# Sixteen weight loads moved from SyncE's DMA queue to GpSimd's, in a kernel that runs a delta-rule attention and an MLP

## The chip, the cores and the metric

The kernel runs on one core of a Trainium2 chip. The metric is the device time of one execution in microseconds (us). A core has five engines with an instruction queue each: TensorE (PE in the profile; its weight loads are PEld), VectorE (DVE), ScalarE (ACT), GpSimd (POOL) and SyncE (SP). Each takes its instructions strictly in order and waits at an instruction until the semaphores that it names have been raised. Transfers between DRAM and the on-chip memory are started by an instruction on SP's, ACT's or POOL's queue and then run by themselves.

## The reference

All inputs are float32 but for the two weight matrices: the set-up scales them by a float64 number, which makes them float64 arrays.

```python
# q, k, v: (4, 8, 768, 48); beta: (4, 8, 768)
k_n = k / (np.linalg.norm(k, axis=-1, keepdims=True) + 1e-06)
state = np.zeros((B, H, D, D))
for t in range(S):
    kt, vt, bt = (k_n[:, :, t], v[:, :, t], beta[:, :, t, None])
    y[:, :, t] = np.einsum('bhd,bhde->bhe', q[:, :, t], state)
    v_old = np.einsum('bhde,bhd->bhe', state, kt)
    state = state + bt[:, :, :, None] * np.einsum('bhd,bhe->bhde', kt, vt - v_old)
x = y.transpose(0, 2, 1, 3).reshape(3072, 384)
h = x @ w_in                                  # w_in: (384, 2048)
g = h * np.clip(h + 3.0, 0.0, 6.0) / 6.0
out = (g @ w_out).astype(np.float32)          # w_out: (2048, 384)
```

## The kernel before

**Tiling.** The 768 tokens are cut into 24 chunks of 32. A chunk of all 4 batches fills 128 partitions (4 x 32). For a chunk the kernel normalizes k (`norms`, then the product `kb` in `prep`, line 496, on POOL), transposes k and q on PE (line 510, tile pt), copies them to the tile KQ on ACT (line 518), forms scores (line 533, tile sc), inverts a small triangular matrix per head, and runs the chain over the state (`chain`: matmul pz at line 813, its copy R on ACT at line 913, the state update su at line 924). Each two chunks make one block of 256 rows for the MLP: `up` (line 980, tile ph) multiplies by w_in, `down` (line 1140, tile po) and for later blocks `down_by_seven` (line 1204) by w_out.

**Weights.** They come as float64 and there is no float64 arithmetic, so they are loaded as pairs of 32-bit words and converted on the chip. The two matrices are cut into 16 pieces: 8 of w_in (384 rows x 256 columns) and 8 of w_out (256 rows x 384 columns), each 768 KB in DRAM. `load_w(i)` (line 312) starts the transfer of piece i into a raw buffer; there are six such buffers, in the tile `spare` and in parts of the tile `w_out` that are not yet in use, and the table `frees` says which earlier piece must have been converted before a buffer is used again. The conversion of a piece is

- three ACT instructions (`scales`, line 337): line 348 scales the high word in its place, line 351 makes a half-precision value of it, line 353 scales the low word; the last two write a carry into `spare`;
- one VectorE shift (`convert`, line 368), from the high word to the final place;
- one GpSimd addition (line 375), which adds the carry there.

**Order.** All of it is recorded under a manual schedule. The string `ORDER` (lines 23 to 41) gives the opening word by word, where `w` stands for the start of one weight piece, `a` for one ACT instruction of `scales`, `c` for one step of `convert`, `k`, `q` and `v` for one load of 48 KB each, and so on; after it a loop over chunks with a table of steps goes on. An engine executes its instructions in the order in which they were recorded. Where a DMA is recorded on a queue, it therefore stands among the other instructions of that engine: on SP among the loads of k, q and v and the stores of the output, on POOL among the masks (line 472), the products (lines 484 and 496), the memsets (lines 277, 285 and 677) and the additions (line 375). In the recorded order the 16 starts stand early: the first before kb's first product, the last after the masks that POOL makes about 112 us into the run before.

DMAs of one queue also share eight semaphores in turn, so the ninth waits until the first has landed; SP's and ACT's DMAs take theirs from one set of eight, GpSimd's would take them from a set of its own.

The lines around the change, without the branch for float32 weights:

```python
raws = []
for i, n in enumerate((0, 1, 2, 3, 4, 5, 0, 1, 3, 4, 5, 0, 1, 5, 0, 1)):
    s, f = weights[i][0].shape[1:]
    raws.append(homes[n].bitcast(U32).rearrange("p (s f z) -> p s f z", s=s, z=2))
frees = {6: 0, 7: 1, 8: 3, 9: 4, 10: 5, 11: 6, 12: 7, 13: 10, 14: 11, 15: 12}
```

Of the kernel before, what the change touches and what calls it, by code (L numbers as in the profile page):

```python
# [44 lines left out]
def kernel(  # L45
# [21 lines left out]
    nc = tc.nc  # L67
# [69 lines left out]
    def needs(*what):  # L137
        assert past.issuperset(what), (what, set(what) - past)
# [173 lines left out]
    def load_w(i):  # L312
        dst, src = weights[i]
        if src.dtype == FP32:
            if i >= NWI:
                needs(("w", NWI - 1))
            nc.sync.dma_start(out=dst, in_=src)
            past.add(("raw", i))
            return
        if i in frees:  # L320
            needs(("seen", frees[i], 0), ("seen", frees[i], 1))
        past.add(("raw", i))
        nc.sync.dma_start(
            out=raws[i].rearrange("p s f z -> p s (f z)"), in_=src.bitcast(U32)
        )

# [1025 lines left out]
    def pieces():  # L1352
        for i in range(NW):
            load_w(i)
            yield
# [166 lines left out]
```

## Time and profile before

| what | value |
|---|---|
| median of 3 runs | 669.1 us (668.65 to 669.87) |
| the profiled execution | 669.61 us, its span 667.8 us |
| PE busy | 635.8 us (95%) |
| VectorE (DVE) busy | 462.8 us (69%) |
| ScalarE (ACT) busy | 260.5 us (39%) |
| GpSimd (POOL) busy | 227.5 us (34%), 336 instructions |
| DMA queue of SP | 31.29 MB in 88,128 packets |
| DMA queue of ACT | 0.30 MB |

The span is what lies between the first and the last instruction of the profiled execution; 1.8 us of its time lie around it. A row of the timeline reads: start in us, duration in us, engine, line of the kernel, operation, output<-input with their shapes, how many merged instructions; in brackets, how long the engine stood idle just before it and what ended that. A `q` behind an engine's name is its instruction queue: the row "SPq L323" is SP starting the DMA of line 323, which takes part of a microsecond; the data land later. The page lists the time from that start to the landing for each kind of DMA:

```profile
spare<-in_moe_w_in_dram SPq DMA_DIRECT2D x4, 768.0 KB, 6.1
w_out<-in_moe_w_in_dram SPq DMA_DIRECT2D x4, 768.0 KB, 6.4
w_out<-in_moe_w_out_dram SPq DMA_DIRECT2D x4, 768.0 KB, 6.9
spare<-in_moe_w_out_dram SPq DMA_DIRECT2D x4, 768.0 KB, 5.7
```

The columns are the tiles, the issuing queue, the count, the size of one, and the median time to landing in us.

### The profile page before, as it was taken

Reading aid. Unit: us, or ns where it says so; the run is one execution under the profiler, and the core shown is the slowest. Engines: PE = TensorE matmul, PEld = TensorE weight load, DVE = VectorE, ACT = ScalarE, POOL = GpSimd, SP = SyncE. Lnnn points to the kernel's source line nnn. Section 1 sums busy time; section 2 is a strip of 40 time slices with the busy share of each in tenths; the row PEclk is TensorE's granted clock in tenths of the full one; section 3 lists DMA queues with packets and bytes.
Section 4 is the critical chain, followed back from the end, with each engine's and each line's share of the span. In section 5 each row is a group of like instructions: output and inputs, shape, how many; then the busy total and the mean of one; then the engine's idle time right before and its main releaser. Section 6 shows DMA issues by size and latency. Waiting matters only on the chain.

```text
span 667.8 us, 26310 instructions
## 1 busy us (share of the span) xinstructions
PE 635.8 (95%) x11544; PEld 568.2 (85%) x11544; DVE 462.8 (69%) x1110; ACT 260.5 (39%) x516; POOL 227.5 (34%) x336
## 2 busy tenths in 40 slices
PE   2768999999999999999999999999999999999997
PEld 2657887776689988988999989999999999999997
DVE  5658653689545687747888857988748998456353
ACT  4765677322142232232244244245244144153250
POOL 5762144202511130363165255055052241331330
PEclk9967999999999999999999999999999999999999
DMA  7887355302040030031030030020020020000000
GB/s 175 201 213 208 77 112 137 69 13 46 17 91 14 3 73 3 2 76 34 3 70 7 2 67 9 2 62 2 3 49 2 2 50 2 19 21 3 26 1 25
DMA packets 88499, 33.27 MB, mean 50 GB/s; under 512 B 80160, under 2 KB 83232, under 8 KB 88384
## 3 DMA queue, kind: packets, MB, share of 16 engines
q1 hardware_dynamic: 88128, 31.29, 20.9%
q8 instruction: 91, 1.49, 0.9%
q10 hardware_dynamic: 256, 0.30, 0.2%
q14 instruction: 24, 0.20, 0.1%
HBM read 26.84 MB, written 4.72 MB: 47 GB/s over the span
## 4 chain that ended last, share of the span: by engine, by line
PE 92%; DVE 2%; SPq 2%; DMA 2%; issue 1%; ACT 1%; DVEq 0%; ACTq 0%
PE po L1204 28%; PE ph L1052 21%; PE ph L980 16%; PE po L1140 6%; PE ks L792 3%; PE pt L510 3%; PE pz L813 3%; PE su L924 3%; PE py L813 3%; PE sc L533 3%; PE yt L859 1%; SPq L168 1%; DMA spare<-in_moe_w_in_dram 1%; PE pi L670 1%; DMA w_out<-in_moe_w_in_dram 1%
## 5 line engine op out<-in xcount | busy, mean ns | idle before, releaser
L1052 PE MATMUL ph<-xT,w_in 128*128 128x128 f32 (+1 forms) x560 | 121.3, 321 | 0.7 <-issue 0.7
L980 PE MATMUL ph<-xT,w_in 128*128 128x256 f32 (+1 forms) x576 | 118.7, 357 | 3.2 <-DVE g L990 2.2
L1204 PE MATMUL po<-w_out,g 128*128 128x192 f32 x640 | 110.6, 326 | 0.0
L980 PEld LDWEIGHTS ph<-xT,w_in 128*128 128x128 f32 x576 | 96.9, 197 | 15.9 <-DVE g L990 2.6
L1204 PEld LDWEIGHTS po<-w_out,g 128*128 128x128 f32 x640 | 104.6, 190 | 0.5
L1052 PEld LDWEIGHTS ph<-xT,w_in 128*128 128x128 f32 x560 | 91.1, 191 | 6.0 <-issue 0.8
L1016 POOL TENSOR_TENSOR g<-g 128x256 f32<-128x256 f32 x112 | 67.9, 608 | 82.9 <-ACT g L1066 78.5
L1204 PE MATMUL po<-spare,g 128*128 128x192 f32 x480 | 86.7, 332 | 0.0
L1204 PEld LDWEIGHTS po<-spare,g 128*128 128x128 f32 x480 | 77.2, 190 | 1.8
L987 ACT ACTIVATE g<-ph,halves 128x256 f32<-128x256 f32 (+1 forms) x96 | 41.8, 437 | 84.6 <-PE ph L980 84.5
L1214 POOL TENSOR_TENSOR o<-o,u 128x192 f32<-128x192 f32 x18 | 13.2, 732 | 175.7 <-ACT o L1211 97.2
L1066 ACT ACTIVATE g<-ph 128x512 f32<-128x512 f32 x56 | 33.5, 597 | 82.2 <-PE ph L1052 82.2
L990 DVE SCALAR_TENSOR_TENSOR g<-g,ph 128x256 f32<-128x256 f32 (+1 forms) x96 | 35.1, 371 | 40.3 <-ACT g L987 40.1
L1190 DVE TENSOR_TENSOR g<-g 128x512 f32<-128x512 f32 x80 | 55.6, 716 | 5.6 <-PE po L1204 5.6
L745 DVE TENSOR_TENSOR pr<-A 128x30 f32<-128x30 f32 (+9 forms) x150 | 57.4, 383 | 2.7
L750 DVE TENSOR_TENSOR A<-A,pr 128x30 f32<-128x30 f32 (+9 forms) x150 | 56.2, 375 | 3.7
L1079 DVE TENSOR_TENSOR g<-ph,g 128x256 f32<-128x256 f32 x56 | 23.5, 420 | 39.0 <-PE ph L1052 32.2
L1211 ACT ACTIVATE o<-po 128x192 f32<-128x192 f32 x40 | 13.2, 331 | 83.2 <-PE po L1204 79.6
L1140 PE MATMUL po<-w_out,g 128*128 128x384 f32 x128 | 45.2, 491 | 0.0
L1093 DVE SCALAR_TENSOR_TENSOR g<-o,g 128x512 f32<-128x512 f32 x56 | 40.7, 726 | 5.9 <-ACT o L1090 5.9
L1090 ACT ACTIVATE o<-g,halves 128x512 f32<-128x512 f32 x56 | 40.4, 722 | 7.6 <-DVE g L1093 5.7
L1052 PE MATMUL ph<-beta_tok,sums_in 128*128 128x128 f32 x224 | 43.3, 275 | 0.0
(144 smaller groups left out, 980.5 us busy)
## 6 DMA issues: line engine op xcount, KB each, us to landing
kf<-in_k_dram SPq DMA_DIRECT2D x96, 48.0 KB, 2.7
qb<-in_q_dram SPq DMA_DIRECT2D x96, 48.0 KB, 2.4
vf<-in_v_dram SPq DMA_DIRECT2D x96, 48.0 KB, 2.0
out_dram<-o SPq DMA_DIRECT2D x92, 48.0 KB, 1.6
spare<-in_moe_w_in_dram SPq DMA_DIRECT2D x4, 768.0 KB, 6.1
w_out<-in_moe_w_in_dram SPq DMA_DIRECT2D x4, 768.0 KB, 6.4
w_out<-in_moe_w_out_dram SPq DMA_DIRECT2D x4, 768.0 KB, 6.9
spare<-in_moe_w_out_dram SPq DMA_DIRECT2D x4, 768.0 KB, 5.7
```

The costliest lines, as they stand in the source:

```text
L745: nc.vector.tensor_tensor(out=pv, in0=A[:, j + 1 :, j].unsqueeze(2).to_broadcast([n, w, j]), in1=A[:, j, 0:j].unsqueeze(1).to_broadcast([n ...
L750: nc.vector.tensor_tensor(out=A[:, j + 1 :, 0:j], in0=A[:, j + 1 :, 0:j], in1=pv, op=ALU.subtract)
L813: nc.tensor.matmul(ps[rows(place(b)), D * h : D * h + D], lhsT=m(h)[rows(b)], rhs=z[rows(b), D * at(h) : D * at(h) + D], start=True, stop= ...
L980: nc.tensor.matmul(ph[:, cols], lhsT=w_in[:, s, f * 128 : (f + 1) * 128], rhs=xT[:, s, cols], start=(s == 0), stop=(s == NKT - 1),)
L987: nc.scalar.activation(out=g, in_=ph, func=ACTF.Relu, bias=half, scale=1.0 / 6.0)
L1016: nc.gpsimd.tensor_tensor(out=out, in0=a, in1=b, op=op)
L1052: nc.tensor.matmul(ph[:, n], lhsT=w, rhs=x, start=start, stop=stop, skip_group_check=True)
L1090: nc.scalar.activation(out=r, in_=g, func=ACTF.Relu, bias=half, scale=1.0 / 6.0)
L1093: nc.vector.scalar_tensor_tensor(out=g, in0=r, scalar=1.0, in1=g, op0=ALU.min, op1=ALU.mult)
L1140: nc.tensor.matmul(pos[c][:], lhsT=gs[blk, f // 2][:, f % 2, c * P : (c + 1) * P], rhs=w_out[:, f, :], start=(f == 0), stop=(f == NFC - 1),)
L1190: nc.vector.tensor_tensor(out=A(f, *out, 4), in0=A(f, *a, 4), in1=A(f, *b, 4), op=op)
L1204: nc.tensor.matmul(ps[n][:], lhsT=A(f - f % 2, *a)[:, f % 2], rhs=b[:, f], start=(f == 0), stop=(f == HF - 1),)
```

## The change

The start of a weight piece is put on GpSimd's DMA queue in place of SyncE's; nothing else is edited. Each of the 16 starts keeps its place in the recorded order, which is now its place among POOL's instructions.

```diff
@@ -320,7 +320,7 @@
         if i in frees:
             needs(("seen", frees[i], 0), ("seen", frees[i], 1))
         past.add(("raw", i))
-        nc.sync.dma_start(
+        nc.gpsimd.dma_start(
             out=raws[i].rearrange("p s f z -> p s (f z)"), in_=src.bitcast(U32)
         )
```

`needs` checks at build time that the instructions which free the buffer have been recorded earlier; the wait itself is a semaphore wait at the DMA's start.

## The prediction

> **What bounds the kernel now.** I read the page first: the slices, then the shares of the chain of waits.
>
> ```profile
> PE   2768999999999999999999999999999999999997
> ...
> PE 92%; DVE 2%; SPq 2%; DMA 2%; issue 1%; ACT 1%; DVEq 0%; ACTq 0%
> ```
>
> From the fifth slice on (16.7 us each) PE is busy to 90% or more, and 92% of the chain is PE. The window view splits that (columns: length, then busy time of PE, PEld, DVE, ACT, POOL, granted clock, DMA share, GB/s):
>
> ```profile
> 0.00:50.00 50.00, 26.75 (x948) 22.43 (x949) 28.25 (x73) 31.91 (x48) 31.82 (x63) 0.90 0.85 196
> ...
> 125.00:667.00 542.00, 538.37 (x8832) 486.29 (x8832) 390.49 (x910) 179.39 (x378) 168.88 (x246) 1.00 0.12 26
> ```
>
> In the first 50 us PE has 23 us idle; after 125 us it has 3.6 us idle in 542. PE takes its work in a fixed order, so a delay that reaches PE in the opening is not made up: it moves the end one for one. All sixteen weight pieces are issued before 108 us, so the question is what the move does to the opening, and there to the engine that converts the pieces ahead of other work, ACT. Its timeline:
>
> ```profile
> 21.72 0.91 ACT L348 ACTIVATE w_out<-w_out 128x768 f32<-128x768 f32 x1 [1.66 <-DMA w_out<-in_moe_w_in_dram]
> 22.51 0.59 ACT L518 ACTIVATE KQ<-pt 128x512 f32<-128x512 f32 x1
> ...
> 32.42 0.90 ACT L348 ACTIVATE w_out<-w_out 128x768 f32<-128x768 f32 x1 [0.89 <-DMA w_out<-in_moe_w_in_dram]
> ...
> 35.50 0.49 ACT L913 ACTIVATE R<-pz 128x384 f32<-128x384 f32 x1
> 38.26 0.89 ACT L348 ACTIVATE w_out<-w_out 128x768 f32<-128x768 f32 x1 [2.27 <-DMA w_out<-in_moe_w_in_dram]
> ...
> 43.50 1.08 ACT L518 ACTIVATE KQ<-pt 128x512 f32<-128x512 f32 x2 [1.11 <-PE pt L510]
> ```
>
> The reader sees that ACT already stands idle until pieces 2, 4 and 5 land (numbering from 0), and that right behind those waits stand the KQ copies and the R copy, without which PE cannot go on with scores and state. A later piece is a later PE.
>
> **When each queue can issue.** SP issued pieces 2, 4 and 5 at these times:
>
> ```profile
> 15.07 0.45 SPq L323 DMA_DIRECT2D w_out<-in_moe_w_in_dram  x1
> ...
> 26.31 0.39 SPq L323 DMA_DIRECT2D w_out<-in_moe_w_in_dram  x1
> ...
> 32.77 0.45 SPq L323 DMA_DIRECT2D w_out<-in_moe_w_in_dram  x1
> ```
>
> In the built order of the changed kernel, POOL's issue of piece 2 stands right behind the addition (L375) of piece 0, that of piece 4 behind the addition of piece 2, that of piece 5 behind the addition of piece 4. Those three additions, before:
>
> ```profile
> 17.24 1.83 POOL L375 TENSOR_TENSOR w_in<-w_in,spare 128x768 int32<-128x768 int32 x1 [1.14 <-ACT spare L348]
> ...
> 26.59 1.83 POOL L375 TENSOR_TENSOR w_in<-w_in,spare 128x768 int32<-128x768 int32 x1
> ...
> 35.48 1.81 POOL L375 TENSOR_TENSOR w_in<-w_in,spare 128x768 int32<-128x768 int32 x1
> ```
>
> They end at 19.07, 28.42 and 37.29, so 4.0, 2.1 and 4.5 us after SP's issue, and each waits for a conversion that itself waits for an earlier piece. The transfers' order stays; a loop closes that was open before: landing, ACT, VectorE, POOL's addition, POOL's issue, landing.
>
> **Unknown: L, from POOL's issue to landing.** The trace of before has no DMA issued by POOL. SP's sixteen pieces took 4.3 / 6.1 / 8.5 us from issue to landing (least, median, greatest, in the view of line 323). Of the issue itself, SP's rows show 0.45 us; on POOL the longest ordinary row is the addition's 1.83, so the issue costs between nothing more than SP's and 1.4 us more. Against it, a queue of its own does not stand behind the k and q loads issued just before (six of them between 7.14 and 10.10 ahead of piece 1). I take L = 6.1, the median, and about 1.1 us of POOL's time in it (the middle of 0.45 and 1.83); both ends, 4.3 and 8.5, go to the range.
>
> **The walk**, s being the lateness gathered so far.
> - Piece 0: POOL is free at 5.29 (end of the memset at 5.08) and waits until 7.32 for VectorE; the issue fits into that gap if it costs under 2.0 us. It lands at 11.4 instead of 12.25 and makes the addition of piece 0 about half a microsecond earlier (ending near 18.5; the rest of the 0.9 is lost to VectorE's own order).
> - Piece 1: behind the masks that end at 11.12, against 10.14 on SP. Lands at 17.2; ACT wanted it at 16.31 and then idled 0.41 before its next instruction. Half a microsecond remains, and is gone in the 1.66 idle before piece 2.
> - Piece 2: issue 18.5, lands 18.5 + L = 24.6; ACT began on it at 21.72. s = L - 3.2 = 2.9. Both KQ copies behind it, and the scores at 24.74, are that late.
> - Piece 3: issued after piece 2 (1.1) and two masks, two products and a memset (2.9), at 22.5, lands at 28.6; ACT, now late, wants it at 26.31 + 2.9 = 29.2. Nothing: the first lateness covers it.
> - Piece 4: issue 28.42 + s = 31.3, lands 37.4; ACT wants it at 32.42 + 2.9 = 35.3. Further L - 4.0 = 2.1; s = 5.0. Behind it the R copy, then PE's state update.
> - Piece 5: issue 37.29 + 5.0 = 42.3, lands 48.4; ACT wants it at 38.26 + 5.0 = 43.3. Further L - 1.0 = 5.1, of which the 1.11 us that ACT idled before the KQ copy at 43.50 is given back: 4.0. s = 9.0.
> - Piece 7: issued after the masks that end at 48.1, lands 48.1 + L, wanted at 50.89: L - 2.8 = 3.3 late, but ACT idled 3.07 before 57.54. Covered but for 0.2; without that cover it costs all 3.3.
> - Pieces 6 and 8 to 15: their distances keep within ACT's idle gaps (piece 8: 48.1 + 6.1 + some 3.7 behind piece 7 against 57.80, even). Piece 15 comes about 4 us later than ACT wants it near 114; PE then has other columns of its order to do, and I count nothing; uncovered it would be 4.
>
> POOL's own 16 x 1.1 = 18 us lies beside that: POOL is busy 31.8 of the first 50 us, and the two products kb (at 28.38 and 37.24) that each stand behind an issue become 1.1 us later than the rest, less than the waits for pieces 4 and 5 that decide there. **Removed from SP**: sixteen issues of about 0.45 us, and its waits. Worth nothing: the loads of k, q and v are early already. ACT waited 3.0 us for k in the first 60 us, 2.6 of it before 4.91 us, ahead of any weight.
>
> **Sum.** (L - 3.2) + (L - 4.0) + (L - 2.1) = 3L - 9.3 = 9.0, and 0.2: 669.6 us of the profiled execution become 678.8. Its time was 0.5 above the median of the runs, so I predict 678.3. L = 4.3 gives +3.6 (672.7), L = 8.5 gives +16.2 (685.3).
>
> The Trainium skill, "DMA: Bandwidth & Descriptors", section "Anatomy of one DMA — SWDGE (gpsimd) path", fits a DMA issued by GpSimd as 2.0 us plus bytes over 436e3 per us. For 786,432 bytes that is an estimate of 3.8 us and would make L so; the sum would then be 0.6 + 0 + 1.7 = 2.3 and the time 671.4, the quick rival below, against 678.3 by the rows. No run so far shows it, and SP's quickest row is 4.3. The same skill, "SBUF — State Buffer", section "SBUF: two separate sides", speaks against the change: such a DMA's descriptors are written by GpSimd's cores and stand still while VectorE holds the port they share. VectorE is busy 28 of the first 50 us here, but its weight shift takes 0.91 us for 768 elements, and no row of before can show whether it would hold up an issue; if it did, that is the slow rival below.
>
> **Rivals.**
> - *Quick landing*: L near 4. With 4.0 the terms are 0.8, 0 and 1.9: +2.7, 671.8. For it: the piece at 93.40 landed in 4.3 with little beside it. Against: the opening moves 196 GB/s, and no piece issued from 5 to 50 us landed in under 5.6 in the view of line 323.
> - *Slow issue*: POOL's part is far over 1.83 us or is held up by VectorE. L = 9 gives +17.7 (686.8), plus piece 0's issue pushing the product at 7.32. For it: POOL takes 0.6 us for a 128x256 product (two masks in 1.19) where VectorE takes 0.42. Against: SP's rows.
> - *Faster: SP's waits were the limit.* The chain begins with the SP queue and runs through pieces 1 and 3, and ACT idled 0.5 + 1.66 + 0.89 + 2.27 = 5.3 us for pieces 1, 2, 4 and 5. Should POOL issue before SP did, that is the gain: 663.8. It decides once POOL's issue comes before 15.07, 26.31 and 32.77. Against: only piece 0 is earlier, by 1.4 us.
> - *Nothing*: lateness stays in idle time; 669. It needs L under 3.3, where the sum is 1.3 or less; no row has that.
>
> **Chances.** Forecast (L from 5 to 8) 0.56; quick 0.17; slow 0.15; faster 0.07; nothing 0.05. A measurement of this kernel tells about 0.2% from no change, 1.3 us. So faster 0.07, within 0.2% 0.05, slower 0.88. The range reaches from between the quick case and nothing, 671, to the slow case's near edge, 686.
>
> **What would show it.** Right: ACT's idle before L348 grows from 6.8 us in the opening to some 16, on pieces 2, 4 and 5; the first scores after piece 2 come about 3 us later, PE's long run at 55.85 about 9; PE's rows after 125 us have the same durations. The issues stand on a new DMA queue with 16 x 768 KB. Wrong: ACT's idle for weights shrinks, PE's lateness differs from 3L - 9.3 with the L that the changed profile shows, or POOL's issue takes the blame through kb instead of through ACT.

## The result

The changed kernel takes 687.5 us (median of 4 runs, 686.0 to 688.2) against 669.5 us (4 runs, 668.7 to 670.2) of the kernel before on the same chip: a ratio of 1.0266, interval 1.0245 to 1.0288. It is slower by 18.0 us. The prediction said slower by 9 us (678.3), with a range to 686.0: the direction was right, the size was half, and the time lies outside the range.

The profiled execution of the changed kernel took 686.0 us with a span of 684.3 (before 669.6 and 667.8), so 16.5 us of span are to be found in it. The slices of PE and the chain of waits on its page answer to those shown of before:

```profile
PE   2545789999999999999999999999999999999997
...
PE 89%; DMA 3%; DVE 2%; issue 2%; ACT 1%; SPq 1%; POOL 1%; DVEq 0%; POOLq 0%; ACTq 0%
```

The chain's share of transfers rises from 2% to 3%, that of "issue" (PE idle though no engine kept it waiting) from 1% to 2%, and POOL enters with 1%: waits that PE's work does not cover. The window view (length, busy time of PE, PEld, DVE, ACT, POOL, granted clock, DMA share, GB/s) puts it into the first 125 us:

```profile
0.00:50.00 50.00, 22.04 (x744) 18.38 (x744) 21.44 (x65) 22.77 (x35) 32.47 (x65) 0.92 0.74 166
50.00:125.00 75.00, 60.62 (x1722) 52.24 (x1721) 44.12 (x118) 47.59 (x89) 29.90 (x33) 0.87 0.46 128
125.00:667.00 542.00, 541.36 (x9000) 485.46 (x8999) 391.39 (x914) 188.39 (x389) 177.09 (x255) 1.00 0.13 28
```

PE had 23.3 us idle in the first 50 before and has 28.0 now; in the next 75 it was idle 4.3 and now 14.4. That is 14.8 us. (After 125 us it idles 0.6 of 542 where it idled 3.6; this window now closes before the end of the kernel.) Over the whole span PE's idle time grew by 14.9 us and its busy time by 1.6 (635.8 to 637.4 on the page), together the 16.5; the longer busy time goes with the granted clock, below.

The loop that the prediction walked is there. POOL's timeline in the changed kernel, an addition (L375) and right behind it the issue of the next piece (L323):

```profile
19.50 1.82 POOL L375 TENSOR_TENSOR w_in<-w_in,spare 128x768 int32<-128x768 int32 x1 [0.64 <-ACT spare L348]
21.26 0.80 POOL L323 DMA_DIRECT2D w_out<-in_moe_w_in_dram  x1
...
32.85 1.83 POOL L375 TENSOR_TENSOR w_in<-w_in,spare 128x768 int32<-128x768 int32 x1
34.61 0.80 POOL L323 DMA_DIRECT2D w_out<-in_moe_w_in_dram  x1
...
44.10 1.80 POOL L375 TENSOR_TENSOR w_in<-w_in,spare 128x768 int32<-128x768 int32 x1 [2.81 <-ACT spare L353]
45.85 0.80 POOL L323 DMA_DIRECT2D w_out<-in_moe_w_in_dram  x1
```

These are pieces 2, 4 and 5 (numbered from 0, as in the prediction). On ACT's timeline the conversions of the same pieces stand with the idle time ahead of each in brackets, and behind them the copies that PE needs:

```profile
27.66 0.88 ACT L348 ACTIVATE w_out<-w_out 128x768 f32<-128x768 f32 x1 [5.35 <-DMA w_out<-in_moe_w_in_dram]
28.44 0.58 ACT L518 ACTIVATE KQ<-pt 128x512 f32<-128x512 f32 x1
...
41.08 0.88 ACT L348 ACTIVATE w_out<-w_out 128x768 f32<-128x768 f32 x1 [2.83 <-DMA w_out<-in_moe_w_in_dram]
...
43.89 0.46 ACT L913 ACTIVATE R<-pz 128x384 f32<-128x384 f32 x1
...
52.49 0.88 ACT L348 ACTIVATE w_out<-w_out 128x768 f32<-128x768 f32 x1 [8.13 <-DMA w_out<-in_moe_w_in_dram]
55.29 2.03 ACT L518 ACTIVATE KQ<-pt 128x512 f32<-128x512 f32 x4
```

5.35 + 2.83 + 8.13 = 16.3 us idle for weights, where the prediction said "some 16". From issue to conversion the three pieces took 6.40, 6.47 and 6.64 us. And PE, idle time in brackets:

```profile
11.83 1.09 PE L510 MATMUL pt<-ident,qb 128*128 128x128 f32 x4 [2.62 <-DMA qb<-in_q_dram]
...
30.65 1.18 PE L533 MATMUL sc<-KQ 64*32 64x64 f32 x64 [4.85 <-ACT KQ L518]
...
44.40 1.30 PE L924 MATMUL su<-R,sums_in 32*64 32x48 f32 x64 [4.62 <-ACT R L913]
...
56.88 2.05 PE L533 MATMUL sc<-KQ 64*32 64x64 f32 x128 [6.49 <-ACT KQ L518]
...
62.45 3.82 PE L980 MATMUL ph<-xT,w_in 128*128 128x128 f32 x18 [0.58 <-ACT xT L863]
...
87.69 0.76 PE L924 MATMUL su<-R,bkb 32*64 32x48 f32 x49 [3.04 <-issue]
```

PE runs the same matmuls in the same order in both kernels, so each can be matched with its own self, and its lateness (start in the changed kernel less start before) followed along the list:

| matmul (start before) | lateness, us | what came in ahead of it |
|---|---|---|
| first transposes of k (8.20) | -0.1 | |
| transposes of q (9.11) | 2.7 | wait for the load of q: **not in the prediction** |
| scores (24.74) | 5.9 | piece 2: +3.2 |
| state update (36.05) | 8.4 | piece 4: +2.5 |
| scores (44.15) | 12.7 | piece 5: +4.4 |
| MLP run (55.85) | 14.6 | half clock: +1.9, **not in the prediction** |
| MLP run (58.6) | 14.1 | |
| state update (70.37) | 17.3 | the 3.04 us of "issue" idle, +3.3: **not in the prediction** |
| 99.75 | 16.5 | given back |
| last matmul | 16.3 | |

The three pieces brought 12.7 - 2.7 = 10.0 us, where the prediction's sum has 9.0. The clock shows in the row at 62.45: the same 18 matmuls took 2.27 us before. The granted clock was 0.5 from 41.8 to 65.7 us and from 72.5 to 75.9 in the changed kernel (27.3 us), and from 34.6 to 44.9 and 55.1 to 61.9 before (17.1 us). Where such a stretch lies on matmuls and not on idle time it costs.

The table picks the places at which PE waits for ACT. Between them the lateness falls, to 5.1 at 40.26, because the kernel before has "issue" waits of its own in the opening, 4.74 us that the changed kernel does not have there:

```profile
34.04 0.27 PE L533 MATMUL sc<-KQ 64*32 64x64 f32 x2 [1.80 <-issue]
...
40.26 0.45 PE L924 MATMUL su<-R,sums_in 32*64 32x48 f32 x3 [2.94 <-issue]
```

That gains nothing, as PE then stands for ACT's late copies instead.

Two things remain to be read: why q comes late and what the 3.04 us are. For q, SP's queue in the changed kernel and POOL's first issue:

```profile
4.96 1.93 SPq L180 DMA_DIRECT2D qb<-in_q_dram  x4
6.93 2.93 SPq L168 DMA_DIRECT2D kf<-in_k_dram  x6
```

```profile
5.24 0.91 POOL L323 DMA_DIRECT2D spare<-in_moe_w_in_dram  x1
```

Before, SP issued piece 0 itself, at 6.65, behind the four loads of q. Now POOL issues it at 5.24, in the middle of them. Taken one by one, the four loads of q are issued at 4.96, 5.46, 5.95 and 6.44 us and land at 7.04, 8.33, 11.44 and 11.70; the piece, issued at 5.24, lands at 11.17. Before, the same four landed at 6.98 to 8.10, each 1.9 to 2.5 us after its issue, and the piece at 12.23. Two loads of 48 KB thus landed behind 768 KB that another engine had issued 0.7 and 1.2 us earlier.

The Trainium skill, "DMA: Bandwidth & Descriptors", section "Issuing engines are not separate DMA queues", says that transfers run on the same 16 DMA engines whichever engine issued them, and that issuing from several saves only the issuing time. This trace agrees, in that a piece of POOL's held up loads of SP's; and what issuing saved on SP, 0.38 to 0.59 us a piece, came back on POOL as 0.72 to 0.91. The Trainium skill, same page, section "Queues, rings and completion order", says that a DMA engine takes packets of the queues in turn. This trace hardly shows such turns: from 8.0 to 9.0 us 87 packets of the piece (4096 bytes each) start and 7 of SP's loads (192 bytes each), while two loads of q are still under way. Whether SP's packets were ready at the DMA engines by then the trace does not tell.

The 3.04 us are idle time of which the profile says that PE waited for no engine. In the changed kernel POOL issues pieces 11 and 12 at 78.48 and 79.34, back to back; before, SP issued them at 58.84 and 67.17. The trace also records the loads of PE's instructions: 91 of 16 KB, which at 256 instructions each (the distance of such waits, as is shown further below) make 23,296, against 23,279 that PE executes. The load that ended this wait started at 85.06 and was through at 86.16, and PE went on at 87.69. PE's instructions were late; whether that is due to the two pieces, 1.5 MB of weights, is for the experiments.

### The profile page after: what moved, and what is told of

The parts are those of the page before. It is cut to its first block, busy times and chain, and to the rows that moved or that the text cites. A ratio compares the mean times of both kernels' runs of the same rounds, so it can differ in the third digit from the quotient of the medians.

```text
span 684.3 us, 26315 instructions
## 1 busy us (share of the span) xinstructions
PE 637.4 (93%) x11544; PEld 569.1 (83%) x11544; DVE 463.7 (68%) x1110; ACT 260.1 (38%) x516; POOL 239.5 (35%) x352
## 3 DMA queue, kind: packets, MB, share of 16 engines
q1 hardware_dynamic: 82752, 18.70, 14.4%
## 4 chain that ended last, share of the span: by engine, by line
PE 89%; DMA 3%; DVE 2%; issue 2%; ACT 1%; SPq 1%; POOL 1%; DVEq 0%; POOLq 0%; ACTq 0%
PE po L1204 27%; PE ph L1052 20%; PE ph L980 15%; PE po L1140 6%; PE ks L792 3%; PE pt L510 3%; PE pz L813 3%; PE sc L533 3%; PE py L813 3%; PE su L924 3%; DMA w_out<-in_moe_w_in_dram 2%; PE yt L859 1%; SPq L168 1%; DVE pr L716 1%; DMA qb<-in_q_dram 1%
```

## The experiments

Each was run beside the kernel before. A ratio is to that kernel's time on the same chip; "lateness" is read as in the table above, from the one profiled execution of each run.

**Piece 0 back on SP**, to see whether the loads of q come back.

```diff
-        nc.gpsimd.dma_start(
+        (nc.sync if i in (0,) else nc.gpsimd).dma_start(
```

> Piece 0 on SP's queue as before, the other fifteen on POOL's. Theory (three causes add up: the loop through POOL's order for pieces 2, 4 and 5; piece 0 landing ahead of the last loads of q for chunk 0, 2.7 us; pieces 11 and 12 issued together, 3.0 us): the q transposes start near 9.1 again and the time falls by some 2.5 us, to 685. Rival (the loop alone sets the opening and swallows what happens before it): no change, 687.5.

Measured: 686.45 us, ratio 1.0228 (1.0180 to 1.0277). The four loads of q land at 7.08 to 8.25 and PE does not wait for them:

```profile
8.08 1.12 PE L510 MATMUL pt<-ident,kb 128*128 128x128 f32 x4 [8.08 <-POOL kb L496]
8.99 1.06 PE L510 MATMUL pt<-ident,qb 128*128 128x128 f32 x4
```

The lateness at the scores of 44.15 falls from 12.7 to 11.2. So the cause of the 2.7 us is shown, but only 1.5 of it reaches past piece 5, and at the end nothing is left of that: this profile has a further half-clock stretch from 85.3 to 95.5 us, behind a 2.81 us "issue" gap, and ends 17.9 late. The intervals of this run and of the whole change overlap, and 686.45 lies between the theory and the rival: by its time alone this run decides nothing.

**Pieces 2, 4 and 5 back on SP**, which opens the loop.

```diff
+        (nc.sync if i in (2, 4, 5) else nc.gpsimd).dma_start(
```

> Pieces 2, 4 and 5 on SP's queue, the other thirteen on POOL's. Theory: the loop is open, ACT's idle for those three pieces falls from 16.3 us to about 5, and of the 18 us only piece 0's 2.7 and the 3.0 of pieces 11 and 12 stay: 675 to 677. Rival (POOL's queue is slow as such, each piece on it costs alike): thirteen sixteenths of 18 us stay, 684.

Measured: 676.89 us, ratio 1.0090 (1.0061 to 1.0120). The first theory holds: some 12 of the 18 us go. On ACT two waits for weights over 1 us are left in the first 75 us, 1.06 and 4.54, and the latter is for piece 6. The lateness is 2.4 at the scores of 24.74 (the loads of q) and 1.9 at those of 44.15. Then the late piece 6 costs what the theory had not named: PE waits 5.99 us for ACT's copy of y, where it waited 1.19 before, and is 5.3 late at the MLP run of 55.85.

```profile
50.98 0.89 ACT L348 ACTIVATE spare<-spare 128x768 f32<-128x768 f32 x1 [4.54 <-DMA spare<-in_moe_w_in_dram]
```

```profile
54.32 0.90 PE L859 MATMUL yt<-ident,y 128*128 128x128 f32 x3 [5.99 <-ACT y L847]
```

The "issue" gap at 70.37 is there again (1.89), and the end is 5.3 late.

**Pieces 11 and 12 back on SP**, which parts the two.

```diff
+        (nc.sync if i in (11, 12) else nc.gpsimd).dma_start(
```

> Pieces 11 and 12 on SP's queue, the others on POOL's. Theory: PE's gap of 3.04 us in the state update near 85 us, in which it waits for nothing that the profile shows, is PE's instructions arriving late behind the two pieces; apart from each other they leave it under 1 us, and the time falls by 2 to 3 us, to 685. Rival (the gap has nothing to do with them): 687.5.

Measured: 684.04 us, ratio 1.0202 (1.0161 to 1.0244). The matmuls that had waited 3.04 us now run without a wait:

```profile
83.39 0.90 PE L924 MATMUL su<-R,bkb 32*64 32x48 f32 x64
```

The end is 14.1 late, 2.2 less than with the whole change. The time of 684.04 is a microsecond below the 685 of the theory.

**Only POOL's time**: all pieces on SP, with six memsets of 128x48 on POOL where the issue stood. Six together take 1.1 us in the trace, somewhat more than an issue's 0.72 to 0.91.

```diff
-        nc.gpsimd.dma_start(
+        for _ in range(6):
+            nc.gpsimd.memset(idle[:], 0.0)
+        nc.sync.dma_start(
```

> All pieces on SP as before; in front of each, POOL writes six small memsets (of a tile that nothing reads), about 0.8 us, as long as its part of an issue. Theory: POOL's time as such lies in its idle gaps, the time stays within 1.5 us of the kernel before. Rival (POOL's 16 times 0.8 us are what the change costs): 6 us or more above it.

Measured: 671.62 us, ratio 1.0009 (0.9979 to 1.0038). What the issues take of POOL costs nothing that can be told; the interval allows 2.5 us at most.

**All pieces on POOL, but 2, 4 and 5 earlier.** In ORDER the word `w` of piece 2 moves to right behind the product kb of chunk 1, that of piece 4 to right behind the addition of piece 1, that of piece 5 behind the addition of piece 3.

```diff
-... n2 k s p1*2 a s*2 ... x0 w q a*3 ... q*2 c*2 x0 ... a w v ... n4 c m3 ... h0 w a*2 ...
+... n2 k s p1*2 w a s*2 ... x0 q a*3 ... q*2 c w c x0 ... a v ... n4 c w m3 ... h0 a*2 ...
```

> All sixteen pieces on POOL's queue, but three of them recorded earlier: piece 2 right behind the product kb of chunk 1, piece 4 behind the addition of piece 1, piece 5 behind the addition of piece 3. Theory (place in POOL's order, not POOL's queue as such): as in the kernel with these three on SP's queue, ACT's idle for them falls from 16.3 us to 5 or less; piece 0's 2.7 us and the 3 us of pieces 11 and 12 stay: 675 to 678. Rival (a piece on POOL's queue is slow wherever it stands): 684 or more.

Measured: 678.77 us, ratio 1.0144 (1.0125 to 1.0164). Half of the loss goes though every piece is still on POOL's queue: the place in POOL's order counts, and not the queue alone. The theory is just missed (678 at most, and 5 us of idle time): ACT's idle time for pieces 2 to 5 is 1.55 + 2.05 + 0.23 + 4.71 = 8.5 us, and piece 5 is the one that stays late.

**Only pieces 2, 4 and 5 on POOL**, the counterpart of the second run.

```diff
+        (nc.gpsimd if i in (2, 4, 5) else nc.sync).dma_start(
```

> The other way round: pieces 2, 4 and 5 alone on POOL's queue, at the places of the change, thirteen on SP's. Theory: the loop alone, by the prediction's own sum with the landing time that the changed kernel shows for these three (6.4, 6.4, 6.6): 3.2 + 2.4 + 4.5 = 10 us, 679 to 681; the q transposes start near 9.1 and no gap of 3 us is left in the state update. Rival (what the opening loses comes from two queues with pieces on both, whichever): under 674, since only three pieces are on the second queue.

Measured: 686.71 us, ratio 1.0276 (1.0237 to 1.0315). **Both expectations are wrong**: these three alone cost as much as all sixteen. POOL's timeline, then SP's queue, then ACT's timeline:

```profile
18.65 0.93 POOL L323 DMA_DIRECT2D w_out<-in_moe_w_in_dram  x1
35.10 0.80 POOL L323 DMA_DIRECT2D w_out<-in_moe_w_in_dram  x1
45.64 0.81 POOL L323 DMA_DIRECT2D w_out<-in_moe_w_in_dram  x1
```

```profile
18.61 0.45 SPq L323 DMA_DIRECT2D w_out<-in_moe_w_in_dram  x1
...
44.39 0.39 SPq L323 DMA_DIRECT2D spare<-in_moe_w_in_dram  x1
44.89 0.42 SPq L323 DMA_DIRECT2D w_out<-in_moe_w_out_dram  x1
```

```profile
28.20 0.88 ACT L348 ACTIVATE w_out<-w_out 128x768 f32<-128x768 f32 x1 [8.48 <-DMA w_out<-in_moe_w_in_dram]
...
40.85 0.90 ACT L348 ACTIVATE w_out<-w_out 128x768 f32<-128x768 f32 x1 [2.12 <-DMA w_out<-in_moe_w_in_dram]
...
55.01 0.88 ACT L348 ACTIVATE w_out<-w_out 128x768 f32<-128x768 f32 x1 [10.86 <-DMA w_out<-in_moe_w_in_dram]
```

SP does not wait for POOL's addition, so pieces that are needed later go ahead: piece 3 at 18.61, in the same moment as piece 2, lands at 24.16, and piece 2 only at 28.17, 9.5 us after its issue. Pieces 7 and 8 stand ahead of piece 5 in the same way, and it takes 9.4 us; piece 4, with nothing large just ahead of it, 5.7. Put into the prediction's three terms, each with its own landing time, that is (9.5 - 3.2) + (5.7 - 4.0) + (9.4 - 2.1) = 15.3 us, and the lateness at the scores of 44.15 is 15.25. So the terms hold and their L is not a property of POOL's queue: it goes with what the DMA engines have been given before, on either queue. It also shows that the parts of this change do not add up: 12 of 18 us go when the three are taken back, yet the three alone cost 17.0 by the medians.

**All named parts mended at once**: the earlier order, and pieces 0, 11 and 12 on SP.

```diff
+        (nc.sync if i in (0, 11, 12) else nc.gpsimd).dma_start(
```

> The early order, and pieces 0, 11 and 12 on SP's queue, thirteen on POOL's. Theory: all three causes are gone; 669 to 672, the time of before within 2 us. Rival (something else of the change is still unfound): 675 or more.

Measured: 674.15 us, ratio 1.0087 (1.0062 to 1.0112), between the two. PE has no "issue" wait at the state update of 70.37 here, but one of 1.85 us at 32.77; ACT waits 3.38 us for piece 2 and 4.61 for piece 5. The lateness is 4.1 at the scores of 44.15 and 4.1 at the end. From the run with the earlier order this one differs by pieces 0, 11 and 12 alone, and is 4.6 us faster: that is the price of the two causes that the prediction did not have, with the loop shortened.

**The earlier places on SP's queue**: the kernel before, with pieces 2, 4 and 5 issued some loads earlier.

```diff
-... x0 w q x0 n1 x0*3 c n2 k s p1*2 a s*2 k q ... x0 w q a*3 ... q*3 a w v ... n4*2 q p2 k b2 h0 c h0 w a*2 ...
+... x0 w q x0 n1 x0*3 c n2 k s p1*2 a s*2 k w q ... x0 q a*3 ... w q*3 a v ... n4*2 w q p2 k b2 h0 c h0 a*2 ...
```

> No GpSimd queue: the kernel before with pieces 2, 4 and 5 each started three or two places earlier on SP, ahead of loads of q that are wanted late. Theory: ACT's 4.8 us of waiting for these pieces in the kernel before is on the path; the time falls by 2 to 4 us, 665 to 668. Rival (the opening is bound by bytes: what the pieces gain the loads lose): no change, 669 to 671.

Measured: 670.73 us, ratio 1.0028 (1.0006 to 1.0050). No gain, rather a loss; the rival's time holds. Its reason is not shown: ACT's waits for pieces 1, 2, 3 and 5 are 0.23 + 0.73 + 1.73 + 2.02 = 4.7 us, where those for 1, 2, 4 and 5 were 5.3, so little was moved, and PE has "issue" waits of 1.94, 2.24 and 1.64 us before 50 us, where it had 1.80 and 2.94.

**All six pieces of the account back on SP**: 0, 2, 4, 5, 11 and 12; the other ten stay on POOL.

```diff
+        (nc.sync if i in (0, 2, 4, 5, 11, 12) else nc.gpsimd).dma_start(
```

> Pieces 0, 2, 4, 5, 11 and 12 are back on SyncE's queue; 1, 3, 6 to 10 and 13 to 15 stay on GpSimd's. Theory (the loss lies in six pieces: 0 through the loads of q, 2, 4 and 5 through their late issue, 11 and 12 through the 3.0 us in which TensorE's instructions are late): 669.5 to 672, no jump over 0.5 us at the opening's transposes or at the su matmul that followed the 3.0 us gap. Rival (any piece on GpSimd's queue delays what SyncE's queue carries beside it, so that the other ten cost too): 674 or more.

Measured: 672.01 us, ratio 1.0024 (0.9996 to 1.0052), at the upper edge of the theory and not told apart from the kernel before. The transposes of q are on time; at the state update of 70.37 an "issue" wait of 0.89 us is left, which the theory put under 0.5. The other ten pieces on POOL's queue cost 1.6 us by the ratio, and no more than 3.5 by its interval. From the run with pieces 2, 4 and 5 on SP this one differs by pieces 0, 11 and 12 alone, and its ratio is lower by 0.66%, 4.4 us: the same price as above.

**Only the late pieces on POOL**: 8 to 15; 0 to 7 are on SP.

```diff
+        (nc.sync if i in (0, 1, 2, 3, 4, 5, 6, 7) else nc.gpsimd).dma_start(
```

> Pieces 0 to 7 are back on SyncE's queue; 8 to 15 stay on GpSimd's. Theory (pieces 11 and 12 issued together put off the fetch of TensorE's instructions by about 3 us, whatever the opening does): 671.5 to 674, with an issue gap of 2 to 3 us at one su matmul near 53 to 56 us. Rival (the gap arose only because the opening was late and the two pieces met a fetch by chance): 669.5 to 671, without the gap.

Measured: 673.07 us, ratio 1.0035 (1.0012 to 1.0058): 2.3 us. The opening is on time (the scores of 44.15 0.1 early), POOL issues pieces 11 and 12 back to back at 64.80 and 65.72, and the gap is there, though the opening was not late. It stands at the same matmuls as with the whole change (70.37 before), at 73.5 us and not near 53 to 56 as was expected:

```profile
73.48 0.74 PE L924 MATMUL su<-R,bkb 32*64 32x48 f32 x48 [2.10 <-issue]
```

The first theory holds in its time and in the gap, which is shorter than its 3 us. The gap does not need a late opening.

## Why the prediction was half right

**The loop**: right in its place, its order and its parts. Pieces 2, 4 and 5 were issued behind the three additions named, ACT idled for those three and, up to 75 us, for no other by more than 0.52 us, the KQ and R copies came late behind them, and after 125 us PE's work took no longer. Taking the three back removes some 12 us; POOL's time alone costs nothing that can be told.

**L**: a term mis-sized. "I take L = 6.1, the median" of SP's pieces; the three took 6.4, 6.5 and 6.6. With these the prediction's sum, 3L - 9.3 with each its own L, gives 10.2, and 10.0 was measured instead of 9.0. But PE ended 16.3 late: by the prediction's own sign of being wrong ("PE's lateness differs from 3L - 9.3 with the L that the changed profile shows") the loop is not all. POOL's issue was taken as 1.1 us and takes 0.8. The quick landing did not come: of the sixteen the least, the median and the greatest time to landing are 4.6, 6.3 and 8.0 us, so the 3.8 us that the prediction estimated from the Trainium skill ("DMA: Bandwidth & Descriptors", section "Anatomy of one DMA — SWDGE (gpsimd) path") is below the least. No issue was longer than 0.91 us on POOL's row, so nothing of the slow issue shows either.

**The failed step** is the removal from SP: "Worth nothing: the loads of k, q and v are early already", together with piece 0, for which the walk counted only that "It lands at 11.4 instead of 12.25". Being issued 1.4 us earlier puts the piece ahead of the last two loads of q, and ahead of them on another queue was here ahead of them on the DMA engines. Before, the last of those loads landed at 8.10 and PE wanted it at 9.11: 1.0 us of cover against 3.6 us of delay, which gives 2.6, and 2.7 was measured. The run with piece 0 on SP shows the cause. What it costs by itself at the end of the kernel was not shown: that run ends no earlier, with a half-clock stretch of its own.

**A second failed step**: "Pieces 6 and 8 to 15: their distances keep within ACT's idle gaps ... I count nothing". ACT was the wrong engine to ask. Two issues that had stood 8.3 us apart on SP's queue came 0.9 us apart on POOL's, and PE stood 3.0 us. The traces show how. Count PE's instructions (matmuls, weight loads and waits) in order of start, from 0: all 38 of its "issue" waits of 0.4 us or more, in the twelve traces, end at number 193 or 194 plus a multiple of 256 (some records may be missing), and 1.2 to 1.6 us after a 16 KB load of its instructions was through. So PE stands at the end of a block of 256 instructions, for the next block. The load that the state update of 70.37 needs is the one that starts after PE has come to number 2497, one block earlier. How long after, and how long PE then waited:

| run | load's start after number 2497, us | PE's wait, us |
|---|---|---|
| before; POOL's time only; 2, 4, 5 alone on POOL; all named parts mended | 0.6 to 0.7 | 0 |
| 11 and 12 on SP | 1.6 | 0 |
| all six on SP | 2.3 | 0.9 |
| earlier places on SP | 2.7 | 1.1 |
| 2, 4 and 5 on SP | 3.4 | 1.9 |
| earlier order on POOL | 3.5 | 2.1 |
| late pieces alone on POOL | 3.6 | 2.1 |
| piece 0 on SP | 4.3 | 2.8 |
| the whole change | 4.4 | 3.0 |

In the last five rows, and in these alone, pieces 11 and 12 were issued back to back within 3 us before that number. That the pieces hold up the load is shown by these runs; how, they do not tell. Nor does it take two pieces: the waits of 1.80 and 2.94 us in the opening of the kernel before stand at such block ends too, behind loads that started 2.2 and 3.1 us after PE had come to the block ahead of it.

**The price.** With the loop open or shortened, taking pieces 0, 11 and 12 back as well saved 4.4 and 4.6 us. By the ratios the 18 us fall into some 12 for pieces 2, 4 and 5, 4.4 for 0, 11 and 12, and 1.6 for the other ten (not told from nothing), in this order of taking back; the parts do not add up in every order.

**The clock** was not in the sum. The lateness grew by 1.9 us between the scores and the MLP, where the clock was half, and 0.5 came back soon. The stretches at half clock differ from run to run, so no run settles what part of the 18 us is theirs, and the difference between two versions of 1 or 2 us cannot be put down to one edit. What is left in the run with all named parts mended, 0.87%, is open in part: its 4.1 us are there by the scores of 44.15, behind ACT's waits for pieces 2 and 5, but 23.9 us are at half clock as well, and what each costs was not tried.

In the profiled execution: 2.7 (q) + 10.0 (loop) + 1.3 (clock) + 3.3 (gap) - 1.0 (given back) = 16.3, the lateness of the last matmul. It was the shortest of the four runs; their median is 1.5 us above it.

## What to carry to other kernels

Moving a transfer to another engine's queue moves its start into that engine's order, so look for what that engine waits for ahead of it, and whether this goes back to an earlier transfer of the same stream. Then list the issues of all queues in one order of time, before and after: whatever is newly issued ahead of a small urgent load can delay it, even from another queue, and an issue that is earlier is not a gain if it overtakes something more urgent. Where large transfers come to stand together, look at what else is being loaded then, the engines' own instructions among it: an "issue" wait of PE can be read from the trace by counting its instructions.

## What was not expected of the hardware

- A 48 KB load that SP issued 0.7 us after a 768 KB piece of POOL's landed behind the piece, 5.5 us after its issue instead of 2.2. With a piece of SP's own and a piece of POOL's issued 0.04 us apart, one took 5.6 us and the other 9.5.
- Two 768 KB pieces issued 0.9 us apart held up a 16 KB load of PE's instructions for 3.4 to 4.4 us where it was 0.6 to 0.7 without, and left PE without work for 1.9 to 3.0 us though no engine was late.
- A 768 KB piece of w_in went in 192 packets of 4096 bytes from POOL's queue and in 384 of 2048 from SP's.
- POOL's issue of a 768 KB transfer took 0.72 to 0.91 us of its timeline, SP's 0.38 to 0.59.
